# Weights loaded step by step, a shared work pool, four q/k buffers and filler matmuls in a fused attention and gated-convolution kernel

## Chip, cores, metric

The kernel runs on one core of one Trainium2 chip. The metric is the device time of the core in microseconds (us), the median of several executions of the same program. The profile is one execution; its "span" is 1.7 to 2.1 us shorter than the time. For a program on one core, the fast or slow state of a run is judged by its time against the fastest run of the same kernel.

## The reference, cut

The program is a hashed attention followed by a gated convolution. Only its structure matters here.

```python
# q, k, v: (4 batches, 8 heads, 768, 64); proj: (64, 6)
q_bucket, k_bucket = hash_bits(q @ proj), hash_bits(k @ proj)      # six sign bits each
scores = q @ k.T / 8, and -1e9 wherever q_bucket != k_bucket
attn   = softmax(scores);   x = attn @ v  -> (4, 768, 512)
p      = x @ w_proj                                                # 512 -> 3 * 512
x1, x2, x3 = thirds of p
conv   = irfft(rfft(x2, axis=1) * rfft(filter_fft, axis=0), axis=1)
out    = (x1 * conv * x3) @ w_out
```

All of it is independent per batch, except that the weights and the filter's spectrum are shared. Two heads together are a "pair": 16 pairs in all, four per batch. The projection of batch 0 needs pairs 0 to 3; the kernel also runs pairs 4 and 5 before it and mixes the others with the projections.

## The kernel before

The kernel records every operation in a list (a `Book`), a small planner (`plan`, `_order`) simulates the engines with its own table of costs and puts the operations into one order per engine, and `issue` emits them in that order. So all instructions of the profile carry one source line, L190 before and L232 after (L229 are the fillers of the change); they are told apart by their tiles. Cuts are marked with `# ...` in code and with `[...]` in diffs, and some comments that explain a line are added.

The path of one pair: load q, k, v; split 16·q and 16·k into a high and a low fp16 part (`hl`, ScalarE and VectorE); transpose them by DMA (`pr_q`, `pr_k`; pair 0 by TensorE instead, `tp`); hash bits on TensorE (`zps`), thresholded on VectorE (`bt`) and written into `pr_q` and `pr_k` by DMA; then 12 score tiles (`stp`, two matmuls each), 12 exps (`pt`, ScalarE), and `pv` matmuls with the values (`vt`).

```python
def nat_load(src, g, which, eng):
    t_ = natp.tile([P, 2 * NCH, HD], FP32, tag="v" if which == "v" else "qk",
                   name=f"nat_{which}", bufs=2)
    # ... eng.dma_start(t_, ...)

def hilo(g):
    for which in ("k", "q"):
        nat = NATS[g][which]
        hl = hlp.tile([P, 2 * NCH, 2, HD], FP16, tag=f"hl_{which}", name="hl")   # one buffer each
        # ... pair 0's q on VectorE:
        nc.scalar.mul(hl[:, :, 0], nat, QKS)
        nc.vector.scalar_tensor_tensor(
            hl[:, :, 1], in0=nat, scalar=QKS, op0=ALU.mult, in1=hl[:, :, 0], op1=ALU.subtract)

def turn_dma(g):
    row = prs[g % NPR]                                                   # three rows
    for which in ("k", "q"):
        nc.sync.dma_start_transpose(row[which]..., HLS[g][which]...)

# in attn_gen, for pair g, half par, tile jt:
    if step == 0 and g + 2 < NG:
        hilo(g + 2); turn_dma(g + 2)
    # ...
    nc.at = g + step / 12.0                                              # priority for the planner
    stp = psS.tile([P, SEQ], FP32, tag="s", name="stp")                  # two buffers
    for lo_c, hi_c in ((0, 512), (512, SEQ)):
        nc.tensor.matmul(stp[:, lo_c:hi_c], kp[kr, ts(jt, P)], qp[kr, lo_c:hi_c])
    nc.scalar.activation(pt[:, 0:SEQ], stp, AF.Exp, bias=nmatch, scale=LSCALE)
```

Weights arrive in fp32 and are split into a high and a low fp16 part. Each piece of work of this setup has a time on the scale of attention steps (4.5 is the middle of pair 4), which is only a priority: a load with nothing before it in its queue starts at once.

```python
def load_p(key, src):
    piece[key] = stg.tile([P, DM], FP32, tag="w32", name="w32", bufs=4)  # one chain of four slots
    nc.sync.dma_start(piece[key], src)

def load_w(c, third, cast):
    src, th, tl = wsrc(c, third)
    if cast:
        nc.gpsimd.dma_start(th, src)                                     # casting load
    load_p((c, third), src)

def split(c, third, cast, eng):
    # ...
    if not cast:
        nc.scalar.copy(th, pc)                                           # high part, ScalarE
    eng.tensor_tensor(tl, pc, th, ALU.subtract)                          # low part

for c in range(NF):
    ev.append((0.9 + 0.1 * c, load_w, (c, 1, True)))                     # third 1 of w_proj
    ev.append((1.6 + 0.4 * c, split, (c, 1, True, nc.gpsimd)))
# ... tables fa, fb at 2.0 to 2.6, ia, ib at 3.0
t_ = T_A                                                                 # 4.5
# ... thirds 0 and 2 of w_proj from t_, then the filter, its folds and
# its spectrum (matmuls hps, evicted by VectorE into hA, hB), then w_out
```

The setup works in a pool of its own (`stg`), which is closed before the pool of the late work (`fl`) is opened.

The softmax here doesn't subtract the row's maximum and nothing guards it: scores larger than these inputs give would overflow.

## Time and profile before

The median is 485.88 us (4 runs, 484.08 to 487.33). The table gives the milestones of the profiled execution (span 482.2 us), read from the timeline of ScalarE's exps.

| before | us |
|---|---|
| first exp | 21.1 |
| last exp of pairs 0 to 5 | 43.9, 61.6, 77.0, 97.7, 109.6, 128.7 |
| first projection matmul (x2a) | 128.2 |
| from there to the end | 354.0 |

The first view is the page's line of groups by busy time: instruction group, busy us, mean ns of one, then the idle time of its engine just before it and what ended most of it.

```profile
L190 ACT ACTIVATE pt<-stp,nmatch 128x768 f16<-128x768 f32 x192 | 167.9, 901 | 90.7 <-PE stp L190 89.5
L190 PE MATMUL stp<-pr_q,pr_k 76*128 76x512 f16 (+1 forms) x384 | 102.0, 351 | 11.9 <-ACT pt L190 9.8
```

An exp takes 0.901 us, and ScalarE scales q and k of each pair (0.843 us each), so ScalarE needs 12 × 0.901 + 2 × 0.843 = 12.5 us per pair. The six pairs took (128.7 − 21.1) / 6 = 17.9 us each. So something other than ScalarE holds the first 128 us.

The second view is the windows view: for each stretch, its length, the busy time of TensorE (PE), its weight loads (PEld), VectorE (DVE), ScalarE (ACT) and GpSimd (POOL) with instruction counts, then the granted TensorE clock, the DMA share and GB/s.

```profile
20.00:40.00 20.00, 10.03 (x46) 3.91 (x46) 6.04 (x10) 8.74 (x11) 1.93 (x1) 0.85 0.58 140
40.00:60.00 20.00, 17.78 (x71) 7.13 (x71) 10.65 (x18) 16.52 (x23) 4.92 (x5) 0.64 0.66 151
60.00:80.00 20.00, 14.49 (x76) 6.60 (x77) 14.47 (x22) 16.16 (x22) 8.96 (x8) 0.88 0.84 194
80.00:100.00 20.00, 15.20 (x73) 6.59 (x72) 12.50 (x18) 11.70 (x15) 12.97 (x11) 0.70 1.06 220
100.00:120.00 20.00, 15.26 (x92) 7.14 (x91) 13.49 (x23) 15.42 (x21) 10.07 (x9) 0.91 0.76 146
128.00:482.00 354.00, 342.34 (x2031) 184.53 (x2029) 230.54 (x438) 172.79 (x250) 46.24 (x42) 1.00 0.32 80
```

After 128 us TensorE is busy 342 of 354 us at clock 1.00: that part is bound by TensorE. In the 100 us before 120 us no engine is full: TensorE is busy for 10.0 to 17.8 of 20 us, ScalarE for 8.7 to 16.5, and the clock is between 0.64 and 0.91. (The DMA share does reach 1.06 from 80 to 100 us.) The clock records of the trace add up to 41 us at half clock before 120 us. The Trainium skill (page "TensorE: Matmul & The Clock Gate", section "The HAM clock gate (the 'warmup' mystery)") says that the clock is either half or full and is set by windows of 3413 ns; the trace agrees, since its pieces at half clock last 3.4, 6.8, 10.2 and 13.7 us.

The third view lists what TensorE waited for up to 130 us: total us, times, longest.

```profile
PE zps L190 <- DMA pr_q<-hl: 14.0, 3, 8.5
...
PE stp L190 <- ACT pt L190: 9.2, 23, 1.0
```

The hash bits wait for transposed q, once for 8.5 us: the transposes of pair 1 were issued at 31.1 and 33.6 us only.

The fourth view is ScalarE's timeline of the start: start us, us, engine (ACTq is its sequencer), tiles, and in brackets the idle time and what ended it.

```profile
4.39 4.74 ACTq L190 DMA_DIRECT2D pj<-in_proj_dram  x2
9.17 1.28 ACT L190 ACT_TABLE_LOAD   x1 [9.17 <-DMA w<-in_moe_w_proj_dram]
10.46 0.84 ACT L190 ACTIVATE hl<-nat_k 128x768 f16<-128x768 f32 x1
...
21.11 4.47 ACT L190 ACTIVATE pt<-stp,nmatch 128x768 f16<-128x768 f32 x5 [7.07 <-PE stp L190]
```

The first exp needs scaled k. That scaling started at 10.46 us, behind a table load that began at 9.17 us. Both stand behind the two small loads of `proj` on ScalarE's own sequencer. The line of the sequencer merges them: they were issued at 4.39 us (0.53 us) and at 8.66 us (0.47 us, until 9.13), and in between the sequencer waited, by the profile's reckoning for a load of weights.

### The profile page before, as it was taken

How to read it: one execution, taken by the hardware profiler on the slowest of the kernel's cores; microseconds unless marked ns; L12 is line 12 of the kernel's file. 1: busy time of each engine (PE TensorE's matmuls, PEld its weight loads, DVE VectorE, ACT ScalarE, POOL GpSimd, SP SyncE). 2: the span in 40 equal slices, each digit the busy share in tenths (PEclk: the TensorE clock that was granted, in tenths of full speed). 3: DMA queues.
4: the chain of work that ended last, by engine and by line, in shares of the span. 5: the costliest groups of instructions: out<-in, count | busy, mean ns of one | idle time of the engine just before them, and what ended most of it. 6: DMA issues, size and time to landing. Idle time of an engine off the chain costs nothing.

```text
span 482.2 us, 6801 instructions
## 1 busy us (share of the span) xinstructions
PE 427.7 (89%) x2464; PEld 222.4 (46%) x2464; DVE 302.7 (63%) x550; ACT 252.9 (52%) x354; POOL 103.4 (21%) x107
## 2 busy tenths in 40 slices
PE   1547875887989989999899899999999999999996
PEld 0213332333435545555455566544455655445652
DVE  2533575675876379944488798723678784158970
ACT  2346776696824665368557475675655652210102
POOL 5512243864511102120212121212121010100000
PEclk9995788598999999999999999999999999999999
DMA  9755889969982231179735144344101010400003
GB/s 255 229 155 128 192 182 191 224 155 184 206 194 74 67 73 33 34 157 247 186 58 128 43 99 108 66 159 107 33 8 33 2 35 23 143 0 1 0 2 130
DMA packets 101905, 52.42 MB, mean 109 GB/s; under 512 B 83704, under 2 KB 93536, under 8 KB 101872
## 3 DMA queue, kind: packets, MB, share of 16 engines
q1 hardware_dynamic: 98976, 50.25, 43.8%
q10 hardware_dynamic: 2256, 1.18, 0.9%
q0 software_dynamic: 640, 0.56, 0.7%
q8 instruction: 19, 0.31, 0.3%
q14 instruction: 14, 0.11, 0.1%
HBM read 33.07 MB, written 6.39 MB: 82 GB/s over the span
## 4 chain that ended last, share of the span: by engine, by line
PE 58%; DMA 16%; DVE 15%; ACT 5%; issue 3%; SPq 2%; POOL 1%; ACTq 0%; DVEq 0%
PE x L190 17%; PE pv L190 9%; PE stp L190 9%; PE wout L190 9%; PE x2a L190 4%; PE x2b L190 4%; DMA pr_q<-hl 4%; ACT pt L190 3%; DMA R<-rdr 3%; PE zps L190 2%; DVE T L190 2%; DMA rdr<-rl 2%; DMA nat_q<-in_q_dram 2%; SPq L190 2%; DVE uv L190 2%
## 5 line engine op out<-in xcount | busy, mean ns | idle before, releaser
L190 ACT ACTIVATE pt<-stp,nmatch 128x768 f16<-128x768 f32 x192 | 167.9, 901 | 90.7 <-PE stp L190 89.5
L190 PE MATMUL stp<-pr_q,pr_k 76*128 76x512 f16 (+1 forms) x384 | 102.0, 351 | 11.9 <-ACT pt L190 9.8
L190 PE MATMUL pv<-pt,vt 128*128 128x257 f16 (+1 forms) x384 | 82.5, 354 | 3.2 <-DVE T L190 3.2
L190 PE MATMUL x<-xh,wph 128*128 128x384 f16 x256 | 83.5, 326 | 0.8 <-DVE T L190 0.7
L190 PE MATMUL x<-xl,wph 128*128 128x384 f16 x256 | 83.5, 326 | 0.0
L190 PE MATMUL x<-xh,wpl 128*128 128x384 f16 x256 | 83.5, 326 | 0.0
L190 PEld LDWEIGHTS <-wph 128*128 128x128 f16 x512 | 49.6, 97 | 35.1 <-issue 3.2
L190 PEld LDWEIGHTS <-pr_k 76*128 76x128 f16 x384 | 38.5, 103 | 56.2 <-issue 30.6
L190 POOL TENSOR_TENSOR xl<-U,xh 128x768 f16<-128x768 f32 x16 | 27.0, 1688 | 164.0 <-DVE xh L190 139.3
L190 PEld LDWEIGHTS <-vt 128*128 128x128 f16 x384 | 39.4, 104 | 36.7 <-issue 11.7
L190 DVE SCALAR_TENSOR_TENSOR T<-S,cst_sb,pv 64x512 f32<-64x512 f32 x64 | 37.7, 608 | 20.9 <-ACT S L190 20.1
L190 ACT COPY S<-pv 64x512 f32<-64x512 f32 (+1 forms) x48 | 22.6, 476 | 43.5 <-PE pv L190 40.0
L190 POOL CAST vt<-nat_v 128x768 f16<-128x768 f32 x16 | 13.2, 822 | 105.6 <-PE pv L190 101.1
L190 DVE TENSOR_SCALAR bt<-zps,cst_sb 128x384 f16<-128x384 f32 x32 | 18.6, 613 | 24.6 <-PE zps L190 24.4
L190 PEld LDWEIGHTS <-wpl 128*128 128x128 f16 x256 | 24.9, 97 | 16.1
L190 PE MATMUL zps<-pr_q,pjh 128*32 128x384 f16 x128 | 16.8, 378 | 17.4 <-DMA pr_q<-hl 14.0
L190 DVE SCALAR_TENSOR_TENSOR U<-T,vsd,R 128x768 f32<-128x768 f32 x16 | 16.6, 1038 | 19.3 <-DMA R<-rdr 19.2
L190 PEld LDWEIGHTS <-xh 128*128 128x128 f16 x192 | 18.7, 97 | 20.8
L190 ACT ACTIVATE osb<-wout 128x512 f32<-128x512 f32 x24 | 14.3, 596 | 24.9 <-PE wout L190 24.8
L190 POOL TENSOR_TENSOR vt<-nat_v,vt 128x768 f16<-128x768 f32 x16 | 26.2, 1640 | 1.2
L190 DVE TENSOR_TENSOR fu<-x2b,x2s 128x512 f32<-128x512 f32 x12 | 8.3, 689 | 22.4 <-PE x2b L190 21.1
L190 DVE SCALAR_TENSOR_TENSOR hl<-nat_q,hl 128x768 f16<-128x768 f32 x16 | 17.5, 1096 | 6.9 <-ACT hl L190 5.4
(329 smaller groups left out, 621.6 us busy)
## 6 DMA issues: line engine op xcount, KB each, us to landing
nat_k<-in_k_dram SPq DMA_DIRECT2D x16, 384.0 KB
R<-rdr SPq DMA_DIRECT2D x32, 192.0 KB
out_dram<-osb SPq DMA_DIRECT2D x24, 256.0 KB
nat_q<-in_q_dram SPq DMA_DIRECT2D x15, 384.0 KB
nat_v<-in_v_dram SPq DMA_DIRECT2D x14, 384.0 KB
w<-in_moe_w_proj_dram SPq DMA_DIRECT2D x12, 256.0 KB
w<-in_moe_filter_fft_dram SPq DMA_DIRECT2D x6, 256.0 KB
w<-in_moe_w_out_dram SPq DMA_DIRECT2D x4, 256.0 KB
```

The source lines that it names most:

```text
L190: o["done"] = getattr(getattr(nc, o["lane"]), o["method"])(*[sub(x) for x in o["args"]], **{n: sub(x) for n, x in o["kw"].items()})
```

## The change

Its intent is to fill the first 128 us: let attention's data go first, keep TensorE's clock up, and free ScalarE. Its parts:

- **Start-up.** ScalarE's table load is pulled to the front (a tiny multiplication ahead of the data), `proj` is loaded by GpSimd's queue, loads for pair 1 move up in the queue.
- **Holds.** Each weight, filter and table load, and the split of each weight, depends on a certain exp (`until`), so that it can't start before that attention step. The order is new too: third 1 of w_proj, then filter and spectrum, then thirds 0 and 2, and w_out and the tables ia and ib last.
- **Casts.** The high part of a weight is cast by VectorE or GpSimd, as the planner finds better (`either`).
- **One shared pool** for setup and late work, four buffers for q and k (`NQK`).
- **Fillers.** 126 matmuls of 256 zero columns, one at the start and 125 put by the planner into gaps of TensorE that it foresees.
- **Planner rules.** Choice of engine, a model of the clock, order rules within a kind of tile (`STREAM`, `FIFO`, `MOST`), new cost figures.

```diff
+    def until(self, t):
+
+        m = [k for a, k in self.marks if a <= t]
+        self.hold = m[-1] if m else None
[...]
-            for k in order:
-                o = self.ops[k]
+            for k, bank in order:
+                if k < 0:
+                    nc.tensor.matmul(self.warm[0](real[bank]), sub(self.warm[1]), sub(self.warm[2]))
+                    continue
+                o = self.ops[k]["form"]
[...]
+BUFS = (5, 6, 5)
+NQK = 4
+WARM_COLS, WARM_UNTIL, WARM_FILL = 256, 115000.0, 0.7
+T_SET = (1.5, 3.0, 5.0)
[...]
+        if o["hold"] is not None:
+            deps[k].add(o["hold"])
[...]
+            gap = s - free[e]
+            if book.warm is not None and s < WARM_UNTIL and gap > 350.0 and before:
+                w0 = free[e]
+                room = w0 + WARM_FILL * gap
[...]
+    one = cp.tile([P, 1], FP32, name="one")
+    nc.vector.memset(one, 1.0)
+    nc.scalar.mul(nmatch, one, -MATCH)
     pj = cp.tile([P, 2, 6], FP32, name="pj")
-    for r0 in (0, HD):
-        nc.scalar.dma_start(pj[r0 : r0 + HD, 0], proj)
     ident = cp.tile([P, P], FP16, name="ident")
     nc.gpsimd.dma_start(ident, id_d.ap())
+    for r0 in (0, HD):
+        nc.gpsimd.dma_start(pj[r0 : r0 + HD, 0], proj)
[...]
-            bufs=2)
+            bufs=2 if which == "v" else NQK)
[...]
-        U = nrm.tile([P, SEQ], FP32, tag="U", name="U", bufs=1)
+        U = R
[...]
-                    stp = psS.tile([P, SEQ], FP32, tag="s", name="stp")
+                    stp = psS.tile([P, 1024], FP32, tag="s", name="stp")
[...]
+                    nc.marks.append((nc.at, len(nc.ops) - 1))
[...]
-            piece[key] = stg.tile([P, DM], FP32, tag="w32", name="w32", bufs=4)
-            nc.sync.dma_start(piece[key], src)
+            piece[key] = stg.tile([P, DM], FP32, tag="xs", name="w32", bufs=NXS)
+            nc.load(piece[key], src)
[...]
-            if not cast:
-                nc.scalar.copy(th, pc)
-            eng.tensor_tensor(tl, pc, th, ALU.subtract)
+            nc.copy(th, pc, "vg")
[...]
+        def both_at(t, load, use):
+            ev.append((t - 0.6, t - 1.0, load[0], load[1:]))
+            ev.append((t, t - 1.0, use[0], use[1:]))
+
         for c in range(NF):
-            ev.append((0.9 + 0.1 * c, load_w, (c, 1, True)))
-            ev.append((1.6 + 0.4 * c, split, (c, 1, True, nc.gpsimd)))
[...]
+            both_at(T_W2 + 0.35 * c, (load_w, c, 1), (split, c, 1))
[...]
-            nc.at, fn, args = events.pop(0)
+            nc.at, t, fn, args = events.pop(0)
+            if t is not None:
+                nc.until(t)
             fn(*args)
+            nc.hold = None
```

## The prediction

> **What bounds the kernel now.** The span is 482.2 us. The windows view splits it. From 120 us on TensorE is busy 350 of 362 us at clock 1.00; counting matmul columns at one per 2.4 GHz cycle, that stretch does 336 us of work, 93% of the possible. In the first 120 us it is busy 77 us, its clock is 0.85, 0.64, 0.88, 0.70, 0.91 in the 20 us windows after the first, and only 47 us of column work is done. Until the first x2a matmul at 128.2 us there is only attention, where ScalarE is the floor: per head pair 12 exps of 0.901 us and two hl scalings of 0.843 us, 12.5 us. The timeline shows six pairs (exps from 21.1 to 128.7 us) at 18 us each. The missing 5.5 us are waits: zps for transposed q/k 14.0 us in all (once 8.5 us: pair 1's q and k were issued at 13 us behind weights and tables), and exps for stp 33 us between 20 and 130 us, partly because stp ran at half clock (0.8 us per tile against 0.32). Start-up takes 21 us: nat_q landed at 6.6 us, but nat_k's scaling on ScalarE began only at 10.5 us, behind weight loads and a 1.28 us table load; small pj/pjh operations added 2 us.
>
> **What the change does.** Removed: four casting weight loads and the weight and table loads of the first 15 us. ScalarE's 16 weight casts (0.6 us each, 10 us) go to DVE/GpSimd; the table load moves ahead of the data. Weight loads wait for an attention step; w_out and ia/ib go behind pair 6; pair 1's q and k are third and fourth in the sync queue. Added: 126 filler matmuls of 256 columns, 13.4 us at full clock, all before the projection, in planned gaps, without waits. Real TensorE work is equal (378.5 us of columns in both orders). The order after pair 6 is nearly the old one, so the last 350 us can gain little.
>
> **Clock.** The Trainium skill (TensorE: Matmul & The Clock Gate, the HAM clock gate) says an idle window of about 3.4 us halves the clock. The trace agrees: about 41 us between 34 and 120 us ran at half, in pieces of 3.4 to 13.7 us. At half clock a pair costs TensorE about 17 us, above ScalarE's 12.5; at full clock 9, below it. So the fillers act on the critical path.
>
> **Sum (estimates from the above).** First exp at about 14.5 us instead of 21.1: -6.5. Six pairs at about 14.3 us (12.5, S copies 1.9 in pairs 4 and 5, residual waits) instead of 18: -22. The projection of batch 0 (about 86% efficient from 130 to 200 us): -3. DMA may take some back: 22.7 MB moved in the first 120 us at share 0.82; in about 100 us the queues are nearly full, so transposes and R may land late.
>
> Predicted: 453 us, 8 in 10 between 439 and 468. Chances: faster by over 2% 0.93, within 2% 0.05, slower 0.02.
>
> **What would show it.** First exp near 14-15 us; first x2a near 98-103 us; clock 0.9 or more in every window after 20 us; zps waits under 5 us; from x2a to the end still about 350 us.
>
> **What would make it wrong.** DMA full: pairs stay at 16-18 us though the clock is full; x1/x3 waiting for late weights in pair 6; DVE and GpSimd casts delaying T and hl.

## The result, and the profile after

The median is 462.38 us (4 runs, 461.61 to 463.65) against 485.88 us. The ratio is 0.9521, 95% interval 0.9477 to 0.9564. Ratios in this document are the mean time of one kernel's fast runs over that of the other's of the same rounds, so not quite the ratio of the medians that are quoted. The span fell by 21.2 us, from 482.2 to 461.0.

| profiled execution, us | before | after | gain |
|---|---|---|---|
| first exp | 21.1 | 15.3 | 5.8 |
| pairs 0 to 3, from the first exp | 76.6 | 56.1 | 20.5 |
| pairs 4 and 5 | 31.0 | 41.4 | −10.4 |
| end of pair 5 | 128.7 | 112.8 | |
| first x2a | 128.2 | 111.9 | |
| from first x2a to the end | 354.0 | 349.1 | 4.9 |

Single pairs took 22.8, 17.7, 15.4, 20.7, 11.9 and 19.1 us before, and 15.9, 12.4, 13.4, 14.4, 25.1 and 16.3 us after (each up to its last exp, from the last exp of the pair before). The sum of the gains, 5.8 + 20.5 − 10.4 + 4.9, is 20.8; the remaining 0.4 us is that the first x2a overlaps the last exps by 0.5 us before and by 0.9 us after. The spectrum explains little of the 4.9 us: before, one of its 24 matmuls ran after the first x2a, now none does.

The same views of the kernel after, first the groups.

```profile
L232 ACT ACTIVATE pt<-stp,nmatch 128x768 f16<-128x768 f32 x192 | 168.6, 899 | 65.1 <-PE stp L232 62.4
L232 PE MATMUL stp<-pr_q,pr_k 76*128 76x512 f16 (+1 forms) x384 | 96.3, 334 | 11.2 <-ACT pt L232 8.5
```

The exps cost what they did. The score matmuls became 5% shorter in the mean (334 ns for 351), which fits the higher clock. The windows view follows.

```profile
20.00:40.00 20.00, 17.37 (x106) 8.23 (x105) 12.22 (x19) 15.98 (x20) 3.39 (x4) 0.82 0.88 197
40.00:60.00 20.00, 15.59 (x117) 8.70 (x115) 14.29 (x26) 16.62 (x21) 7.31 (x8) 1.00 0.75 194
60.00:80.00 20.00, 17.65 (x122) 10.15 (x119) 15.65 (x23) 18.02 (x24) 17.05 (x13) 1.00 0.85 229
80.00:100.00 20.00, 15.20 (x75) 6.43 (x75) 14.30 (x26) 8.62 (x13) 5.46 (x7) 0.80 0.89 195
100.00:112.00 12.00, 11.39 (x77) 6.39 (x76) 10.14 (x18) 10.50 (x15) 4.13 (x4) 0.90 0.65 168
112.00:461.00 349.00, 339.96 (x2012) 184.36 (x2011) 227.36 (x421) 171.59 (x247) 68.33 (x61) 1.00 0.32 82
```

From 40 to 80 us the clock is full and ScalarE busy 16.6 and 18.0 of 20 us: there the kernel comes near the floor of ScalarE. From 80 to 100 us, in pair 4, ScalarE is busy for 8.6 of 20 us only, as little as in the poorest window of before. What TensorE waited for, up to 115 us, has changed as well.

```profile
PE stp L232 <- ACT pt L232: 8.5, 16, 4.0
PE zps L232 <- DMA pr_q<-hl: 4.2, 4, 1.9
```

The waits for transposed q and k shrank from 14.0 to 4.2 us. The wait for exps that must empty a score bank stayed at about 9 us, but its longest is now 4.0 us; it lies in pair 4. Last, the start on ScalarE.

```profile
1.25 1.28 ACT L232 ACT_TABLE_LOAD   x1 [1.25 <-PEq L1368]
...
4.19 0.84 ACT L232 ACTIVATE hl<-nat_k 128x768 f16<-128x768 f32 x1 [1.44 <-DMA nat_k<-in_k_dram]
...
15.28 1.69 ACT L232 ACTIVATE pt<-stp,nmatch 128x768 f16<-128x768 f32 x2 [2.98 <-PE stp L232]
```

The table load runs before any data is there, and k is scaled at 4.19 us, 6.3 us earlier than before. The Trainium skill (page "ScalarE: Activation LUTs", section "What ACT_TABLE_LOAD costs") gives 1283 ns for the load and 1380 ns more of drain for a switch to a different set of functions. The trace agrees on the load, 1.28 us in both kernels. The program has this one load and no switch, and the next instruction follows after 0.01 us in each kernel, so no run here shows the drain.

### The profile page after: what moved, and what is told of

The parts are those of the page before. It is cut to its first block, busy times and chain, and to the rows that moved or that the text cites. A ratio compares the mean times of both kernels' runs of the same rounds, so it can differ in the third digit from the quotient of the medians.

```text
span 461.0 us, 7071 instructions
## 1 busy us (share of the span) xinstructions
PE 431.6 (94%) x2590; PEld 233.4 (51%) x2590; DVE 305.9 (66%) x552; ACT 252.8 (55%) x348; POOL 112.2 (24%) x117
## 4 chain that ended last, share of the span: by engine, by line
PE 71%; DMA 12%; DVE 9%; ACT 3%; issue 3%; SPq 1%; DVEq 0%; ACTq 0%; POOLq 0%
PE x L232 24%; PE pv L232 10%; PE stp L232 9%; PE wout L232 9%; PE x2b L232 6%; PE x2a L232 6%; DMA pr_q<-hl 4%; PE zps L232 2%; DMA lt<-S 2%; ACT pt L232 2%; DMA w<-in_moe_w_proj_dram 2%; PE fdft L232 2%; DMA pr_k<-hl 1%; DMA R<-rdr 1%; DMA rdr<-rl 1%
## 5 line engine op out<-in xcount | busy, mean ns | idle before, releaser
L232 PE MATMUL stp<-pr_q,pr_k 76*128 76x512 f16 (+1 forms) x384 | 96.3, 334 | 11.2 <-ACT pt L232 8.5
L232 PE MATMUL pv<-pt,vt 128*128 128x257 f16 (+1 forms) x384 | 76.4, 333 | 1.4 <-DVE bt L232 1.4
L232 PEld LDWEIGHTS <-pr_k 76*128 76x128 f16 x384 | 36.9, 99 | 49.8 <-issue 22.8
L232 POOL TENSOR_TENSOR xl<-R,xh 128x768 f16<-128x768 f32 x16 | 26.3, 1641 | 133.1 <-DVE xh L232 112.4
L232 PEld LDWEIGHTS <-vt 128*128 128x128 f16 x384 | 37.8, 99 | 29.8 <-issue 5.9
L232 ACT COPY S<-pv 64x512 f32<-64x512 f32 (+1 forms) x48 | 22.8, 476 | 43.1 <-PE pv L232 39.1
L232 PEld LDWEIGHTS <-wpl 128*128 128x128 f16 x256 | 25.0, 97 | 16.1
L232 PEld LDWEIGHTS <-xh 128*128 128x128 f16 x192 | 18.7, 97 | 20.7 <-issue 0.3
L232 DVE TENSOR_SCALAR bt<-zps,cst_sb 128x384 f16<-128x384 f32 x30 | 17.5, 610 | 16.2 <-PE zps L232 15.7
L232 ACT ACTIVATE osb<-wout 128x512 f32<-128x512 f32 x24 | 14.3, 596 | 24.7 <-PE wout L232 24.6
L232 POOL CAST vt<-nat_v 128x768 f16<-128x768 f32 x11 | 9.0, 823 | 74.1 <-PE pv L232 74.1
L232 DVE SCALAR_TENSOR_TENSOR R<-T,vsd,R 128x768 f32<-128x768 f32 x16 | 16.2, 1012 | 14.6 <-DMA R<-rdr 14.6
L232 DVE SCALAR_TENSOR_TENSOR hl<-nat_k,hl 128x768 f16<-128x768 f32 x16 | 16.3, 1016 | 12.2 <-ACT hl L232 12.1
L232 ACT ACTIVATE hl<-nat_k 128x768 f16<-128x768 f32 x16 | 13.5, 844 | 14.7 <-DMA pr_k<-hl 9.1
```

Source lines behind the costliest of these rows:

```text
L232: o["done"] = getattr(getattr(nc, o["lane"]), o["method"])(*[sub(x) for x in o["args"]], **{n: sub(x) for n, x in o["kw"].items()})
```

## The experiments

Twelve kernels ran. Each was timed in the same rounds as the kernel before, whose medians were 485.21, 486.96 and 487.83 us in the three sets, each on another chip. "Replanned" below means that an edit gave the planner another problem, so that it may have moved other things too; e1 is the one that leaves the order of all other instructions as it was.

| run | edit | median us | before us | ratio [95%] |
|---|---|---|---|---|
| e1_no_fill | change without fillers | 462.98 | 485.21 | 0.9535 [0.9497, 0.9573] |
| e2_before_fill | before with 310 fillers | 491.58 | 485.21 | 1.0113 [1.0061, 1.0165] |
| e6_no_hps | change without filter spectrum (wrong result) | 455.47 | 485.21 | 0.9382 [0.9333, 0.9431] |
| e7_before_hold | before, weights held until first exp | 489.78 | 485.21 | 1.0079 [1.0042, 1.0116] |
| e3_act_cast | change, weight casts on ScalarE | 459.08 | 486.96 | 0.9421 [0.9383, 0.9459] |
| e4_nqk2 | change with two q/k buffers | 466.91 | 486.96 | 0.9580 [0.9538, 0.9622] |
| e5_no_hold | change without holds | 472.53 | 486.96 | 0.9691 [0.9646, 0.9737] |
| e9_before_table | before with early table load | 480.66 | 486.96 | 0.9864 [0.9819, 0.9909] |
| e10_before_hold_filter | e7, filter ahead of thirds 0 and 2 | 480.29 | 487.83 | 0.9850 [0.9805, 0.9895] |
| e11_act_cast_no_fill | e3 without fillers | 462.80 | 487.83 | 0.9491 [0.9454, 0.9528] |
| e12_early_filter | e11, filter at step 2.5 | 464.95 | 487.83 | 0.9549 [0.9507, 0.9592] |
| e13_earlier_filter | e11, filter at step 2.0 | 461.52 | 487.83 | 0.9465 [0.9427, 0.9503] |

### e1: do the fillers matter?

The claim under test is the prediction's "the fillers act on the critical path". The rival: the stretch is paced by ScalarE and the DMA queues, so a half clock costs nothing there.

```diff
                 if k < 0:
-                    nc.tensor.matmul(self.warm[0](real[bank]), sub(self.warm[1]), sub(self.warm[2]))
                     continue
```

> The changed kernel with its 125 fillers dropped when the program is issued, so that the order of every other instruction is unchanged. Theory A (load order and start-up make most of the gain, the fillers a small part): 464 to 469 us, first exp still near 15.5 us, half-clock time before the projection up from 30 us (20 us after the first 27 us) by 10 us or more. Theory B (the clock makes most of the gain): 473 us or more, with pairs 0 to 5 back near 18 us each.

The ratio is 0.9535 against 0.9521 for the change: the same within the intervals. The median is below even the range of theory A. In the profile the clock fell and the six pairs together did not get slower (the windows of e1).

```profile
20.00:40.00 20.00, 16.34 (x82) 6.60 (x81) 9.91 (x16) 13.07 (x16) 1.51 (x3) 0.65 0.79 192
40.00:60.00 20.00, 15.07 (x91) 7.50 (x91) 15.64 (x27) 18.46 (x24) 7.91 (x9) 0.95 0.79 171
60.00:80.00 20.00, 16.14 (x103) 8.03 (x103) 15.88 (x23) 16.12 (x21) 15.55 (x12) 0.88 0.86 227
80.00:100.00 20.00, 15.98 (x70) 6.26 (x70) 16.55 (x28) 10.35 (x15) 7.99 (x9) 0.74 0.84 201
```

The clock records add up to 41 us at half clock before x2a, as in the kernel before, and to 20 us in the change (they begin at 10 us in both, at 27 us in the kernel before). From 20 to 40 us the clock is 0.65 instead of 0.82. Yet the six pairs took 96.1 us (15.7 to 111.8), against 97.5 us with fillers, and the first x2a came at 111.0 us instead of 111.9. Pairs 1 and 3 did lose (16.0 and 16.5 us, 12.4 and 14.4 with fillers), but the others made it up. So at this place in this plan the fillers are worth nothing that three rounds can show. TensorE waited longer for exps to free score banks (11.6 us after 8.5): part of what the fillers fill is time in which it has to wait anyway. The other executions say the same: e1's profiled run had a mean clock of 0.956 and took 462.29 us, its three others had 0.972 to 0.976, near the change's 0.976 to 0.980, and took 462.31 to 465.00 us.

The three profiles (before, change, e1) also show when the clock falls. Before the first x2a it fell 14 times. In the 3.4 us before each fall, TensorE was busy for 0 to 62% of the time. Only one fall (before, at 34.0 us) followed a stretch without any work; before the others the longest single gap was 0.4 to 3.0 us. In the 3.4 us before each return to full, TensorE was busy for 84 to 100%. So here the clock followed how busy TensorE was, and a half clock does not mean that it stood still.

### e2: fillers alone, in the kernel before

```diff
+GAPS = {0: 40, 12: 12, 24: 10, [...] 326: 3, 369: 12}   # matmul -> fillers ahead of it
[...]
+                        if mm > 1 and not half and left_ > 0:     # behind each of the first 72 score tiles
+                            left_ -= 1
+                            for _ in range(2):
+                                nc.tensor.matmul(last[:, SEQ:1024], sub(self.warm[0]), sub(self.warm[1]))
```

> The kernel before with 310 fillers only: two after each score tile of the first six pairs and some in each wait of over 0.35 us that its trace shows, nothing else moved. Theory A: 479 to 486 us, because the waits for transposed q/k and loads stay (clock near 1.0 from 10 us on, but pairs still over 16 us). Theory B: 465 to 475 us.

It became 1.1% slower, outside both forecasts, and the trace points to the experiment's own placement. The fillers write into the spare columns of the score bank, so an exp is released only after them. ScalarE's timeline of this run shows it (L212 are the fillers behind a score tile).

```profile
57.41 0.90 ACT L200 ACTIVATE pt<-stp,nmatch 128x768 f16<-128x768 f32 x1 [0.23 <-PE stp L212]
59.33 0.90 ACT L200 ACTIVATE pt<-stp,nmatch 128x768 f16<-128x768 f32 x1 [1.02 <-PE stp L212]
```

Up to 138 us, exps waited 40.5 us with those fillers as the releaser (before, 32.8 us for the score matmuls up to 130 us). Nor was the clock kept up: 31 us ran at half clock before the first x2a. So this run says what badly placed fillers cost; it does not tell what fillers in true gaps would bring to the kernel before. That stays untested there.

### e6: is it the filter spectrum that makes pair 4 long?

In the trace of the change, pair 4 holds the work on the filter: four `s`, `r` folds on VectorE, 24 `hps` matmuls, and their evictions. VectorE's timeline in pair 4 of the change:

```profile
78.88 1.89 DVE L232 TENSOR_TENSOR s<-fu 128x512 f16<-128x512 f32 x1
...
83.31 0.75 DVE L232 TENSOR_SCALAR hA<-hps,cst_sb 128x512 f32<-128x512 f32 x1
...
85.29 0.95 DVE L232 SCALAR_TENSOR_TENSOR hl<-nat_k,hl 128x768 f16<-128x768 f32 x1
86.16 0.95 DVE L232 SCALAR_TENSOR_TENSOR hl<-nat_q,hl 128x768 f16<-128x768 f32 x1
```

The `hl` step of pair 6 is ready (ScalarE's part was done at 75.5 and 77.8 us), but runs at 85.3 and 86.2 us, behind the folds and the first evictions. The transposes follow it: the queue's own timeline has them at 86.71 and 90.43 us. The exps stood still meanwhile, first for score matmuls that came behind `hps`, then behind a scaling of k:

```profile
84.12 0.90 ACT L232 ACTIVATE pt<-stp,nmatch 128x768 f16<-128x768 f32 x1 [3.23 <-PE stp L232]
...
94.88 0.84 ACT L232 ACTIVATE hl<-nat_k 128x768 f16<-128x768 f32 x1 [3.60 <-DMA rdr<-rl]
```

TensorE then waited 3.97 us for the exp behind that scaling. (The profile names a small DMA, rdr, as the releaser at 94.88 us. The tile `hl` of k has one buffer, which the transpose issued at 86.71 us still reads; which of the two it was is not settled.)

```diff
-                ev.append((t_ + 0.2 * i - 0.6, t_ + 0.2 * i - 1.0, load_f, (n,)))
-            if fn is not None:
-                ev.append((t_ + 0.2 * i, None, fn, a))
[...]
-        hps = Feed(hps_gen(f))
+        hps = Feed(iter(()))
+        hfake()      # hA, hB, hD filled with a constant, early
```

This kernel is wrong (relative error 2.28).

> The changed kernel with a wrong result on purpose: the filter spectrum (filter loads, low tables, folding on GpSimd and VectorE, 24 hps matmuls, their evictions) is left out and constants take its place. It tells why pair 4 took 25 us instead of the 14.3 us that I had predicted. Theory P (the hps work and the order it forces on VectorE, ScalarE and the sync queue stall pair 4): pair 4 falls to 14 to 16 us, first x2a at 98 to 103 us, 449 to 453 us. Rival Q (DMA is full around pair 4, from weights of thirds 0 and 2 and q/k/v): pair 4 stays at 19 us or more, 456 us or more.

Pair 4 took 13.5 us instead of 25.1, and pairs 0 to 5 ended at 31.6, 43.6, 58.4, 72.1, 85.6 and 99.9 us. VectorE's `hl` for the same pair ran at 75.3 and 78.8 us and its transposes were issued at 80.59 and 82.30 us, 6 to 8 us earlier than in the change:

```profile
75.26 0.95 DVE L232 SCALAR_TENSOR_TENSOR hl<-nat_k,hl 128x768 f16<-128x768 f32 x1
...
78.81 1.58 DVE L232 SCALAR_TENSOR_TENSOR hl<-nat_q,hl 128x768 f16<-128x768 f32 x1
```

So the spectrum is the cause of the long pair 4; which of its loads, folds, matmuls and evictions does it, this run does not separate. But its removal did not bring those 12 us, and the median is above the 449 to 453 us of theory P. The first x2a came at 108.3 us, only 3.6 us earlier, because two other waits took over (the chain of waits before x2a):

```profile
97.67 5.47 DMA pr_q<-hl
...
103.19 1.47 PE zps L232 x16
...
105.63 1.96 PE stp L229 x10
```

The transposed q was 5.47 us on its way, TensorE stood 2.9 us for it, the clock fell, and ten fillers at half clock (2.17 us) then ran in the way of real work. From x2a on, 345.2 us were left, 3.9 less than in the change; the kernel was replanned, and this is not explained. Nor is e6 a bound for a correct kernel: the 24 `hps` matmuls must run somewhere. At 0.216 us each, the distance at which the x2a matmuls of 512 columns follow each other in the trace, they are 5.2 us.

### e5: what are the holds worth?

```diff
-            if t is not None:
-                nc.until(t)
+            nc.hold = None
```

> The changed kernel without the holds: weight, filter and table loads may be issued as soon as a buffer is free, as in the kernel before (planned again; q/k/v of pairs 0 and 1 still come first in the queue). Theory E (the holds keep the DMA queues free for q/k in the first pairs): 468 us or more, pairs 1 and 2 at 16 us or more instead of 12.5 and 13.4. Rival: 460 to 465 us.

The first exp came at 15.1 us, as in the change, but the first x2a at 126.5 us instead of 111.9: almost the whole early gain went. (This profiled execution, 476.21 us, is the slowest of five, 3.7 us above their median.) Pairs 1 and 2 took 27.3 and 16.1 us, as theory E forecast. The sync queue shows the delay. Without holds, filter loads (and, before these lines, weights and tables) stand ahead of the transposes of pair 2:

```profile
22.91 3.33 SPq L232 DMA_DIRECT2D w<-in_moe_filter_fft_dram  x4
...
31.21 1.44 SPq L232 DMA_TRANSPOSE pr_k<-hl  x1
...
34.84 1.50 SPq L232 DMA_TRANSPOSE pr_q<-hl  x1
```

With holds, the same transposes were issued about 12 and 6 us earlier:

```profile
19.51 2.42 SPq L232 DMA_TRANSPOSE pr_k<-hl  x1
...
28.36 1.44 SPq L232 DMA_TRANSPOSE pr_q<-hl  x1
```

The place in the queue is not all of it. A transpose needs `hl`, and in e5 VectorE runs `hl` of pair 2 just before these transposes:

```profile
33.85 0.96 DVE L232 SCALAR_TENSOR_TENSOR hl<-nat_q,hl 128x768 f16<-128x768 f32 x1 [0.95 <-ACT hl L232]
```

Before that, the exps had stood for 5.7 us, until pair 1's hash bits had their transposed q. That transpose was issued at 19.25 us and took 6.26 us to land (18.05 us and 4.62 us in the change); VectorE split weights just before it, and the DMA share of the first 20 us was 0.99 (0.88 in the change). So early loads delay q and k, as theory E says. How much is due to busy DMA engines, to the early splits, and to the new plan, is not separated.

The cost is (0.9691 − 0.9521) × 486 = 8 us by the ratios, 10 us by the medians (472.53 against 462.38). This is the largest of the parts that were taken out one by one. The Trainium skill (page "DMA: Bandwidth & Descriptors", section "Issuing engines are not separate DMA queues") says that all DMAs run on the same 16 engines and interleave; no run here tests this by itself, but it fits the shares above: what the holds choose is what these engines carry first.

### e7 and e10: the load plan alone, in the kernel before

e7 holds the weight, filter and table loads until the first exp, and changes nothing else.

```diff
+                    if nc.first is None:
+                        nc.first = len(nc.ops) - 1          # the first exp
[...]
+            nc.hold = nc.first
             fn(*args)
+            nc.hold = None
```

> The kernel before with one thing changed: weight, filter and table loads may not be issued before the first exp is done (the planner then also puts the filter spectrum behind pair 5). No fillers. Theory A: 468 to 478 us, first exp at 15 to 17 us, the zps wait of 8.5 us of pair 1 gone. Theory B: 481 us or more.

It became 0.8% slower. The early part did gain: first exp at 18.3 us (21.1 before), first x2a at 122.8 us (128.2 before). But all loads of the setup go through one chain of four slots, in order. Held at the front, the filter came at 95 to 115 us instead of 70 to 85, its spectrum at 153 to 165 us, inside the projection, and from x2a to the end took 365 us instead of 354. Nor did the waits for transposed q and k go: they were 10.8 us, and pair 1 took 23.7 us (17.7 before), since all loads are let go together at the first exp. So a hold needs an order of loads that goes with it. e10 adds that order: filter and spectrum ahead of thirds 0 and 2 of w_proj.

```diff
-        t_ = T_A
-        [... thirds 0 and 2 ...]
-        t_ += 0.9
+        t_ = 3.0
         [... filter, spectrum ...]
-        t_ = t_hps + 0.4
+        t_ = 5.0
+        [... thirds 0 and 2 ...]
```

> The kernel before with the load plan alone: the holds of e7 (no weight, filter or table load before the first exp is done) and, as in the change, the filter loads and the filter spectrum ahead of weights of thirds 0 and 2, so that the spectrum stays out of the projection. Casts, buffers, pools and fillers as before. If e7 failed only because the holds pushed the spectrum into the projection (153 to 165 us): 466 to 474 us, hps over before 110 us, first x2a at 112 to 118 us. If the holds gain only together with the four q/k buffers and the new planner rules: 479 us or more.

The ratio is 0.9850, 1.5% faster than before; the median lies in the rival's range. The spectrum now ran at 78 to 95 us. The first x2a came at 118.0 us, 10.2 us earlier, but it is no fair milestone here: the planner put it ahead of the rest of pair 5, whose last exp came at 138.5 us. Pair 6 ended at 164.8 us instead of 171.4, 6.6 us earlier; the spans of the two profiles differ by 3.1 us. Pair 1 again took 23.9 us, with a wait of 5.2 us for transposed q. So this load plan alone, with one hold for all loads instead of a step for each, gives about a third of the change's 4.8%; holds are worth more together with the other parts.

### e3: casts back on ScalarE

The claim: taking the weight casts off ScalarE helps, since ScalarE is the floor of the attention stretch. Mind the count: the kernel before had 12 casts on ScalarE, not 16, so e3 puts four more there than before.

```diff
-            nc.copy(th, pc, "vg")
+            nc.copy(th, pc, "s")
```

> The changed kernel with the 16 casts of the weight split put back on ScalarE (planned again). Theory C (ScalarE is the floor of the early pairs, so moving the casts off it was worth most of their 10 us): 468 to 472 us. Rival (the early pairs have slack on ScalarE because they wait for DMA and other engines): within 3 us of the changed kernel, 459 to 466 us.

This kernel is faster than the change: 459.08 us, ratio 0.9421 with an interval that ends at 0.9459, below the 0.9477 at which that of the change begins. The first x2a came at 108.6 us instead of 111.9; pair 4 took 21.5 us instead of 25.1, pairs 1 to 3 about the same. Theory C is out. So this part of the change, as planned here, cost some 1% (3 to 5 us, by medians and by ratios) instead of helping. The kernel was replanned, though, and e9 below shows that another plan alone can shift some microseconds; so the sign of the casts' own effect is not certain. A plausible reason, argued and not shown by a run of its own: on VectorE and GpSimd, work of the two engines that overlaps slows each other. e9's start shows how much. The first line is VectorE, the second GpSimd, of the same stretch.

```profile
9.74 2.20 DVE L190 SCALAR_TENSOR_TENSOR hl<-nat_k,hl 128x768 f16<-128x768 f32 x1
```

```profile
9.50 1.63 POOL L190 TENSOR_TENSOR vt<-nat_v,vt 128x768 f16<-128x768 f32 x1
```

The same `hl` instruction takes 0.95 us when GpSimd is silent (shown under e6, at 85.29 us of the change). The Trainium skill (page "SBUF — State Buffer", section "Who interferes with whom") says that a VectorE instruction with two SBUF inputs contends with a GpSimd instruction that reads SBUF, and that "PE and ACT never wait on anyone". The trace agrees on the first, 2.20 us against 0.95 us. By the second, ScalarE's casts stand outside of this; in e3 the twelve of w_proj took 0.61 to 0.64 us each.

### e4: two q/k buffers

```diff
-NQK = 4
+NQK = 2
```

> The changed kernel with two instead of four q/k buffers (planned again). Theory D (early loads of q and k, made possible by the buffers, take the waits for transposed q/k off the early pairs and are the main gain): 472 us or more, zps waits back over 10 us before the projection. Rival: 466 us or less, zps waits stay under 6 us.

The ratio is 0.9580 against 0.9521: the buffers are worth about 0.6%, 3 us (4.5 us by the medians), between what the two theories said, and the intervals overlap. The direction is seen in the profile: first exp 16.8 us, first x2a 116.6 us, and waits of the hash bits for transposed q and k 8.1 us instead of 4.2. The opposite experiment, the kernel before with four buffers, did not build: a pool needed 24.5 kB per partition and 23.16 kB were left. So the buffers need room that the kernel before does not have, and the change makes room by the shared pool and by R and U in one tile; the shared pool's own effect on time can't be told apart.

### e9: the early table load alone, in the kernel before

```diff
-    for r0 in (0, HD):
-        nc.scalar.dma_start(pj[r0 : r0 + HD, 0], proj)
[...]
+    for r0 in (0, HD):
+        nc.gpsimd.dma_start(pj[r0 : r0 + HD, 0], proj)
[...]
-    nc.vector.memset(nmatch, -MATCH)
+    one = cp.tile([P, 1], FP32, name="one")
+    nc.vector.memset(one, 1.0)
+    nc.scalar.mul(nmatch, one, -MATCH)
```

> The kernel before with two small changes of the start alone: ScalarE's table load is brought ahead by a tiny multiply at the start and the two proj loads are issued by GpSimd. Weight loads stay early. If the table load and the late pj operations set the first exp: first exp at 18 to 19 us instead of 21.1, 482 to 484 us. If the weight loads ahead of q and k set it (nat_k landing): first exp 20 to 21 us, 485 us as before.

ScalarE scaled k at 4.22 us instead of 10.46, and yet the first exp came at 20.7 us, 0.4 us earlier only. VectorE did q first, then `hl` of k took 2.20 us beside GpSimd's work on the values (the two lines shown under e3), and the small cast `pjh` took 1.07 us beside GpSimd's weight splits, as in the kernel before; in the change, where GpSimd is idle from 11.05 to 12.37 us, it takes 0.17 us. VectorE's lines of that cast, before and after:

```profile
15.00 1.07 DVE L190 CAST pjh<-pj 128x12 f16<-128x12 f32 x1
```

```profile
11.11 0.17 DVE L232 CAST pjh<-pj 128x12 f16<-128x12 f32 x1
```

So the table load and the `proj` loads alone do not bring the 5.8 us of the start; in e7, the holds alone brought 2.8 of them. That the rest comes from the free GpSimd and from all of it together is argued from these lines. This kernel was 1.4% faster than before all the same, and in the profile all of that lies after x2a: the first x2a came 1.3 us later (129.5 us), and 350.2 us followed instead of 354, where the edit has no direct effect. It was replanned; why the late part gained is not settled.

### e11, e12, e13: a better version?

e3 was the best so far, and e1 had said that fillers do nothing. So e11 takes both, and e12 and e13 move the filter's spectrum to earlier pairs.

```diff
 e11:  [e3's edit and e1's edit]
 e12:  -T_SET = (1.5, 3.0, 5.0)   +T_SET = (1.5, 2.5, 5.0)     on top of e11
 e13:  -T_SET = (1.5, 3.0, 5.0)   +T_SET = (1.0, 2.0, 5.0)     on top of e11
```

> The changed kernel with weight casts on ScalarE (as e3) and no fillers (as e1). If the fillers do nothing in e3's plan either: 458 to 460.5 us, equal to e3. If fillers that land on TensorE's critical path cost something, as in e6: 455 to 458 us. If they help once ScalarE carries more: 461 us or more.

> e11 with the filter stage half an attention step earlier (T_F 2.5 instead of 3.0). The planner then puts the first x2 matmuls ahead of pair 5's last scores. If the spectrum's place is what delays the projection: first x2a before 106 us and 453 to 458 us. If the transposes and normalisation of pairs 3 to 6 delay it: 458 to 462 us.

> e11 with weights of third 1 half a step earlier and the filter stage one step earlier (T_SET 1.0, 2.0, 5.0): the whole spectrum then falls in pair 3. Earlier loads compete with q/k of pairs 1 to 3. If e5's loss came from that competition: pairs 1 and 2 over 14 us and 461 us or more. If there is room: pair 4 at 14 to 15 us and 453 to 458 us.

e11 measured 0.9491, against 0.9421 for e3 (on another chip, each against its own runs of before; the interval of e3 ends at 0.9459 and that of e11 begins at 0.9454, so they just meet). In that plan the fillers may be worth 0.7%, unlike in the change; the clock hardly differs (mean of the runs 0.979, 0.982 in e3). e12 gave 0.9549, no gain and above both forecasts: the spectrum ran from 77 us, and pair 5 ended at 128.2 us, after the first x2a at 106.5. e13 gave 0.9465: pair 4 fell from 21.5 to 12.7 us, but pair 3, where the spectrum now lies (69.8 to 78.2 us), rose from 18.7 to 20.3, pairs 1, 2 and 5 rose by 4.7 together, and the first x2a came at 107.8 us (110.4 in e11). So pair 4 is short wherever the spectrum is elsewhere, as in e6, and other pairs take back most of it. None of them beat e3, which beats both kernels at 459.08 us.

## Why the prediction was right, and where it was wrong

The prediction was 453 us (439 to 468), faster with a chance of 0.93; the result is 462.38 us, inside the range and above its middle by 9 us. Part of this is luck: the range is wide, two of the causes that it names (the clock and the casts) brought nothing in the runs, and what carried the gain it had listed without a price.

- **The floor and the place of the gain: right.** The gain lies before the first x2a (16.3 us of 21.2). From there to the end, 349.1 us was measured and "about 350" predicted.
- **Start, "−6.5": measured −5.8.** First exp at 15.3 us, predicted 14.5.
- **"Six pairs at about 14.3 us instead of 18: −22": measured −10.1. This is the mis-sized term.** Pairs 0 to 3 fit it well (56.1 us, 14.0 each). Pairs 4 and 5 took 41.4 us instead of 28.6. The sum had put only the `S` copies into them; it left out the filter's spectrum. Before, 19 of its 24 matmuls ran between 119 and 128 us, in pair 5, which took 19.1 us; the change moves all of them into pair 4. e6 showed it: without the spectrum pair 4 takes 13.5 us. With it came a first x2a at 111.9 us, where 98 to 103 was predicted.
- **"So the fillers act on the critical path": wrong.** The premise was that at half clock a pair costs TensorE about 17 us, above ScalarE's 12.5. e1 ran at half clock for 41 us and was as fast as the change. The 17 us are the work of a pair that runs wholly at half clock, but the pieces at half clock lasted 3.4 to 13.7 us, and each fall came where TensorE had been busy for 62% of the time or less. They lay next to time to spare; that nothing was lost because of it is argued. (The prediction's 0.8 against 0.32 us for a score tile also mixes two measures: by the timeline a tile alone takes 0.81 us at half and 0.48 us at full clock.) By what taking parts out cost, the pairs' gain came mostly from what the prediction had listed without pricing: the holds (e5: 8 to 10 us) and the buffers (e4: about 3 us).
- **"Clock 0.9 or more in every window after 20 us": wrong.** 0.82, 1.00, 1.00, 0.80, 0.90. By e1, no loss of time that shows followed from it.
- **Casts off ScalarE, seen as a gain ("ScalarE's 16 weight casts … go to DVE/GpSimd"): no gain, and miscounted.** The trace of before has 12 casts on ScalarE (6.9 us), and ScalarE took over five casts of `vt` (4.1 us) in the change. e3 is faster with the weight casts on ScalarE. The last item of "what would make it wrong", casts that delay T and hl, named the danger.
- **"zps waits under 5 us": right,** 4.2 us.
- **Tail, "−3": measured −4.9.** What brought it was not tested.

What stays open: how the holds' 8 to 10 us come about (DMA engines, early splits or plan); whether e3's 1% is the casts' own; why replanned kernels differ by some microseconds after x2a (e9, e10); whether fillers help in e3's plan; what the planner's new rules and the shared pool bring by themselves. The parts also don't add up by design: each was measured by taking it out of a plan that was made with the others.

## What to carry to other kernels

When no engine is full in an early stretch, look first at what delays its small transfers: holding bulk loads back, and with them the work that they release, was worth more than any other part taken out here (e5), provided that the loads' own order (e7 against e10) and the other parts fit it. Price each piece of work where the new order puts it, also work that did not change, such as the spectrum in pair 4. And a low clock is no loss by itself: drop the fillers from the finished order and time it, as e1 did, before counting on them.

## What the Trainium skill lacked or had wrong

- "TensorE: Matmul & The Clock Gate", section "HAM oscillation — how this bites in real kernels": beside its rule against idle gaps of over 3.4 us it lacks the share of busy time at which short gaps alone bring the clock down (here 13 of 14 falls followed 3.4 us with TensorE busy for 12 to 62% and no gap over 3.0 us), and when a full clock pays. Here the fillers raised the mean clock of four runs from 0.970 (e1) to 0.978 and changed the time by 0.1% (462.98 to 462.38 us), within the noise; fillers in front of an exp's release cost 1.1% (e2).
- "ScalarE: Activation LUTs", section "What ACT_TABLE_LOAD costs": its 1283 ns agree (1.28 us); it gives the drain for a switch and lacks what follows a first load. Here the next instruction starts 0.01 us after the load's end.
- "SBUF — State Buffer", section "Who interferes with whom": it has the rule, but no sizes for instructions like these. A cast of 128x12 took 1.07 us beside GpSimd and 0.17 us without it, and a two-input step of 128x768 took 2.20 us against 0.95.
- "DMA: Bandwidth & Descriptors": it lacks how long a transpose between SBUF tiles takes behind bulk loads. Here transposed q was 5.47 us on its way in e6, with the DMA share at 1.01 from 97 to 103 us, and in the change the sync queue was held for 1.3 to 2.5 us per transpose.
